# Spreading the range tests of the weights over a pair's turns on ScalarE, with a fourth raw buffer

## Chip, cores and metric

The kernel runs on one core of a Trainium2 chip. The metric is the device time of one execution in microseconds, as the median of several runs. A core has five engines that run at the same time and wait for each other by semaphores: PE (matrix multiply), VectorE (DVE in the profile), ScalarE (ACT), GpSimd (POOL) and SyncE (SP), which here only issues DMAs.

## The reference

Two blocks follow each other. The first is attention with routing: every query and every key is given to the nearest of 16 centroids of its head, and a query sees only the keys of its own cluster. The second is a feed-forward layer with a sigmoid approximation of GELU.

```python
# q, k, v: (4, 8, 768, 64); centroids: (8, 16, 64)
q_assign = argmax(einsum('bhsd,hcd->bhsc', q_n, c_n), axis=-1)
k_assign = argmax(einsum('bhsd,hcd->bhsc', k_n, c_n), axis=-1)
mask = q_assign[:, :, :, None] == k_assign[:, :, None, :]
scores = where(mask, scale * matmul(q, k.T), -1e9)
attn = softmax(scores)
x = matmul(attn, v)                     # bridged to (3072, 512)
h = x @ w_in                            # w_in: (512, 2048)
g = h * (1 / (1 + exp(-1.702 * h)))
return g @ w_out                        # w_out: (2048, 512)
```

The weights are given as 64-bit floating-point numbers; q, k, v and the centroids as 32-bit ones.

## The kernel before

The order of all work on every engine is written out by hand in program order: nothing is reordered. The tile layer adds the semaphores, and a tile's buffer is used again when all readers and writers of its former content are done.

**The attention stage** goes over 16 pairs of heads. A pair has two halves of 384 queries, and a half has six key tiles of 128 keys; a *unit* `u` is one key tile of one half, for both heads of the pair. The main loop takes two units in a *turn* `t`. So there are 96 turns, three to a half and six to a pair (`TG = 3`), and two more that finish. In the text a turn's number is `t % 6`, its place in the pair. In a turn, on each engine in this order:

- PE: `scores` of the turn's units (L467) into the PSUM tiles `s`, of which there are as many as a turn needs; `part` (L490, L481 in the first pair), which adds the cluster codes held in `rows`; then `values` (L532) of the turn before; in turns 1 and 4 the row sums (L549); in turn 1 the distances of the next pair to the centroids (`prep_near`, L343).
- ScalarE: `exps` (L498), the exponentials of `s` into `A`; then `check` (L584, L586, in turns 2 and 5), which tests the reciprocals of the row sums; then the copies of the output out of PSUM (L541, in turns 0 and 3); then, where a weight chunk was made in this turn, its test.
- VectorE: the transposes of q and k of the next pair (L322, turn 0), one addition of `A` to the row sums (L509, turn 0), the normalisation of a half (L559 to L571, turns 1 and 4), the cluster assignment of the next pair (L366 to L403), and the weight rounding (L189 to L207).
- GpSimd: the other additions of `A` to the row sums (L516), four instructions to most turns.
- SP: the loads of q and k (`in`, L134), v (L144) and the weights (`raw`, L170), the spreading of the cluster codes over rows (L412, L418), and stores of finished tiles (`kept`, L575).

The scores of the next turn overwrite `s`, so they wait for the exponentials of this turn. `A` has four buffers, each read by PE (L532) and added to the row sums.

**The weights** come in 32 chunks of 128 x 512 numbers. `rounding` turns a chunk from its raw 64-bit form into 32-bit floating point in five VectorE instructions (`steps = (0, 0, 0, 5, 0, 5)`: one whole chunk in turns 3 and 5 of a pair, besides three chunks in turns 3, 4 and 5 of the first pair). It begins with the load of the chunk two further on. It ends with `check_w`, the range test: two ScalarE instructions, a square with a sum along the row (L231) and an exponential of it with a second sum (L234). Each issues one more, short instruction that reads the accumulator. Their results go to a scratch tile `z` and are of no use; the sums go to `row_sums`. For 31 chunks `z` is the place of the last chunk in `w_out`, which is not written yet; for the last chunk it is every second word of the raw tile itself. Raw tiles have three buffers. At the end of the kernel the sums decide whether a general version must run after it; with these inputs it does not.

**The feed-forward stage** (from about 347 us) multiplies in block forms that save products. Its tiles take the memory of the attention's pools, which `att.close()` sets free; the first to be written is `G`, by a ScalarE copy (L855).

Of the kernel before, what the change touches and what calls it, by code (L numbers as in the profile page):

```python
# [8 lines left out]
FP32 = mybir.dt.float32  # L9
# [4 lines left out]
AF = mybir.ActivationFunctionType  # L14
# [24 lines left out]
def fast(  # L39
# [26 lines left out]
    nc = tc.nc  # L66
# [28 lines left out]
        name="spill", bufs=1, space=bass.MemoryType.DRAM))  # L95
# [1 line left out]
    ctx.enter_context(tc.manual_schedule())  # L97

    att = ExitStack()
    wp = att.enter_context(tc.tile_pool(name="wp", bufs=3))  # L100
    inp = att.enter_context(tc.tile_pool(name="inp", bufs=3))
    pairs = att.enter_context(tc.tile_pool(name="pairs", bufs=2))
    asg = att.enter_context(tc.tile_pool(name="asg", bufs=2))
# [5 lines left out]
        name="dram", bufs=2, space=bass.MemoryType.DRAM))  # L109
# [3 lines left out]
    def bank():  # L113
        return ps_m.tile([P, 512], FP32, name="m")
# [26 lines left out]
    def load_v(p):  # L141
# [16 lines left out]
    w_chunks = [  # L158
        (w[:, c, n:n + WN],
         src.bitcast(I32)[c * P:(c + 1) * P, 2 * n:2 * (n + WN)])  # L160
        for w, src, n_c, n_n in ((w_in, moe_w_in, NCH, DF),
                                 (w_out, moe_w_out, NF, DM))
        for n in range(0, n_n, WN) for c in range(n_c)]
    NW = len(w_chunks)
    w_raw, w_pow = {}, {}

    def load_w(i):
        if i < NW:
            t = wp.tile([P, WN, 2], I32, name="raw")
            nc.sync.dma_start(out=t.rearrange("p n t -> p (n t)"),  # L170
                              in_=w_chunks[i][1])
            w_raw[i] = t
# [7 lines left out]
    def rounding():  # L180


        i = w_done[0]
        load_w(i + 2)
        raw, w = w_raw.pop(i), w_chunks[i][0]
        e = wp.tile([P, WN], I32, name="e", bufs=2)
        a = bank()
        hi, lo, a_i = raw[:, :, 1], raw.bitcast(U32)[:, :, 0], a.bitcast(I32)
        nc.vector.tensor_scalar(out=a_i, in0=hi, scalar1=3, scalar2=0x3FFFFFF8,  # L189
                                op0=ALU.logical_shift_left,  # L190
                                op1=ALU.bitwise_and)
        yield
        nc.vector.scalar_tensor_tensor(out=a_i, in0=hi, scalar=ODD, in1=a_i,
                                       op0=ALU.bitwise_and, op1=ALU.bitwise_or)
        yield
        nc.vector.tensor_scalar(out=e, in0=a_i, scalar1=POWER, scalar2=None,
                                op0=ALU.bitwise_and)
        yield
        e = e.bitcast(FP32)
        nc.vector.scalar_tensor_tensor(out=e, in0=lo, scalar=2.0 ** -52, in1=e,  # L200
                                       op0=ALU.mult, op1=ALU.mult)
        yield
        if i >= NW // 2:
            w, a, e = (w.rearrange("p (n r t) -> p r n t", r=P // SQ, t=SQ),
                       *(x.rearrange("p (r n t) -> p r n t", r=P // SQ, t=SQ)
                         for x in (a, e)))
        nc.vector.tensor_tensor(out=w, in0=a, in1=e, op=ALU.add)  # L207

        check_w(i, raw, w_chunks[NW - 1][0] if i < NW - 1 else raw.bitcast(
            FP32)[:, :, 1])  # L210
        w_done[0] += 1
        yield

# [2 lines left out]
    def step():  # L216

        if not now and w_done[0] < NW:
            now.append(rounding())
        if now:  # L220
            n = w_done[0]
            next(now[0])
            if w_done[0] > n:
                now.clear()

    def check_w(i, raw, z):

        nc.scalar.activation(out=z, in_=raw.bitcast(FP32)[:, :, 1],  # L231
                             func=AF.Square,
                             accum_out=row_sums[:, 2, i:i + 1])
        nc.scalar.activation(out=z, in_=z, func=AF.Exp, scale=-2.0 ** 12,  # L234
                             bias=fifteen[:, 0:1],
                             accum_out=row_sums[:, 3, i:i + 1])

    load_qk(1, 0)
    load_v(0)
# [7 lines left out]
    half, fifteen, top, css, cnorm, crec = (  # L247
        consts[:, i:i + 1] for i in range(6))
# [20 lines left out]
    row_sums = const.tile([P, 4, NW], FP32, name="sums")  # L269
# [19 lines left out]
    def keep_busy(n):  # L289
        for _ in range(n):  # L290
            nc.tensor.matmul(
                out=idle[:, 0, :], lhsT=ident_h,
                rhs=ident_h[:, None, :].broadcast_to((P, 4, P)),
                start=True, stop=True)
# [5 lines left out]
    for a in range(2):  # L300
        rows = slice(a * D, (a + 1) * D)
        nc.vector.tensor_copy(
            out=cT[rows, :, a, :],
            in_=cps[rows, 0:P].rearrange("d (h a c) -> d h a c", a=2,
                                         c=NC)[:, :, a, :])
# [154 lines left out]
    def scores(u):  # L460
        g, kt = divmod(u, NJ)
        p, h = split(g)
        ps = ps_s.tile([P, 2, 512], FP32, name="s")
        for a in range(2):
            rows = slice(a * D, (a + 1) * D)
            for c in range(0, P, D):
                nc.tensor.matmul(  # L467
                    out=ps[c:c + D, a, 0:HALF],
                    lhsT=T[p, 1][rows, kt * P + c:kt * P + c + D],
                    rhs=T[p, 0][rows, h * HALF:(h + 1) * HALF],  # L470
                    start=True, stop=False)
        s_of[u] = ps[:, :, 0:HALF]

    def part(u):

        g, kt = divmod(u, NJ)
        p, h = split(g)
        if p == 0:
            for a in range(2):
                r = SQ * a  # L480
                nc.tensor.matmul(  # L481
                    out=s_of[u][:, a, :],
                    lhsT=hots[1][r:r + NC, kt * P:(kt + 1) * P],
                    rhs=hots[0][r:r + NC, h * HALF:(h + 1) * HALF],
                    start=False, stop=True)
            return
        for a in range(2):
            rows = slice(a * D, (a + 1) * D)
            for c in range(0, P, D):
                nc.tensor.matmul(  # L490
                    out=s_of[u][c:c + D, a, :],
                    lhsT=rows_of[1, p % 2][rows, kt * P + c:kt * P + c + D],
                    rhs=rows_of[0, p % 2][rows, h * HALF:(h + 1) * HALF],
                    start=False, stop=True)
# [85 lines left out]
    def check(g):  # L580


        rec = recs.pop(g)
        nc.scalar.activation(out=rec, in_=rec, func=AF.Copy,  # L584
                             accum_out=row_sums[:, 0, g:g + 1])
        nc.scalar.activation(out=rec, in_=rec, func=AF.Relu, bias=top[:, 0:1],  # L586
                             scale=-2.0 * LIMIT * LIMIT,
                             accum_out=row_sums[:, 1, g:g + 1])
# [49 lines left out]
    TG = NJ // 2  # L638

    prep_at = {}  # L640
    for p in range(1, NPAIR):
        for i in range(2 if p == 1 else 0, len(PREP)):
            t = 2 * TG * (p - 1) + (0, 0, 0, 0, 1, 2, 2)[i]
# [5 lines left out]
    def prep(p, i):  # L649
        if i == 2 and p:  # L650
            load_v(p)
        PREP[i](p)
        if i in (1, 3) and loads:
            load_qk(*loads.popleft())
# [9 lines left out]
    for t in range(NT + 2):  # L664
        us = range(2 * t, 2 * t + 2) if t < NT else ()
        for u in us:
            scores(u)
        if t == 0:
            keep_busy(6)
            prep(0, 6)  # L670
            keep_busy(4)
        for u in us:
            part(u)
        for u in us:
            exps(u)
        if recs:
            check(*recs)
        for u in us:
            add_up(u)
        if t == NT - 1:  # L680
            sums_w(0)
            sums_w(1)
        work = sorted(prep_at.get(t, ()), key=lambda w: PREP[w[1]] != prep_near)
        turns = [w for w in work if w[1] < 4]
        for p, i in turns:
            prep(p, i)
        work = [w for w in work if w[1] >= 4]
        while later:
            later.pop()()
        if 1 <= t <= NT:  # L690
            for u in range(2 * t - 2, 2 * t):
                values(u)
        if t >= 2 and (t - 2) % TG == TG - 1:
            row_sums_of((t - 2) // TG)
        while work and PREP[work[0][1]] == prep_near:
            prep(*work.pop(0))
        if t >= NT - 8 and t < NT:
            XT = list(next(made))
        for p, i in work:
            prep(p, i)  # L700
        for _ in range(0 if t in (0, 1, 2, NT - 1) else 5 if t == 4 else
                       steps[t % (2 * TG)]):
            step()
        if t >= 2 and (t - 2) % TG == TG - 1:
            normalise((t - 2) // TG)
    check(*recs)
    att.close()


# [277 lines left out]
    for b in range(B):  # L987
# [18 lines left out]
        if b < B - 1:  # L1006
            for h in range(2):
                for hp in range(HP):
                    x = xT_of[b + 1, h, hp] = xp.tile([P, HALF], FP32,
                                                      name="x")  # L1010
# [491 lines left out]
```

## Time and profile before

| | |
|---|---|
| three runs | 909.20, 909.56, 909.67 us; median 909.56 |
| the profiled execution | 909.0 us, its span 907.1 us |
| PE | 887.9 us busy, 98% of the span |
| VectorE | 728.6 us, 80% |
| GpSimd | 492.3 us, 54% |
| ScalarE | 363.4 us, 40% |
| granted clock of PE | 0.996 |
| attention stage, 58.6 to 140.8 us | of 82.2 us: PE 81.7, VectorE 75.1, GpSimd 75.6, ScalarE 58.1 |
| range tests, chunks 0 to 30 | L231: 31 of mean 688 ns; L234: 31 of mean 722 ns |
| range test, chunk 31, in place | L231: 709 ns; L234: 769 ns |

The span runs from the first to the last instruction; the execution's own time has some 1.9 us around it. Matmuls are pipelined and their ends are modelled, so a PE that is busy for 98% of the span can still be held up by others: whether it is can be read from the chain of waits, which goes back from the last instruction to what released it, step by step. A timeline lists one engine's instructions with their start, their length, and, in brackets, how long the engine was idle before and what ended the idle time.

### The profile page before, as it was taken

To read this page: it belongs to the slowest core of one execution; us is meant where nothing else is said; L and a number is where in the kernel's file an instruction comes from. 1 tells how busy PE (TensorE), PEld (TensorE's weight loads), DVE (VectorE), ACT (ScalarE), POOL (GpSimd) and SP (SyncE) were. 2 spreads that over 40 slices of the span, in tenths; PEclk is the share of its full clock that TensorE was granted. 3 is DMA by queue.
4 is the path that set the end of the run, shared out by engine and by line. 5 is a ranking of instruction groups with operands and counts; after the bars stand their busy time and mean duration, and the time that the engine had idled before them with its cause. 6 is when DMAs were issued, how large, how long until landed. Compare 5 with 4: busy or idle time off the path is not lost.

```text
span 907.1 us, 17734 instructions
## 1 busy us (share of the span) xinstructions
PE 887.9 (98%) x6712; PEld 578.1 (64%) x6712; DVE 728.6 (80%) x1170; ACT 363.4 (40%) x816; POOL 492.3 (54%) x469
## 2 busy tenths in 40 slices
PE   8999999999999999999999999999999999999995
PEld 3444444444444445557996557997557997557994
DVE  4999999998899997998898556797556797556894
ACT  3767767777676773322111232112232112232110
POOL 5899889998999998694275221143221143220120
PEclk9999999999999999999999999999999999999998
DMA  9465556666565210036213202322202322200323
GB/s 182 119 122 110 102 119 131 143 138 132 125 142 121 85 43 18 0 117 232 70 53 106 52 1 70 102 63 98 52 1 70 104 56 103 52 1 1 104 58 86
DMA packets 177565, 78.97 MB, mean 87 GB/s; under 512 B 154440, under 2 KB 160704, under 8 KB 177472
## 3 DMA queue, kind: packets, MB, share of 16 engines
q1 hardware_dynamic: 176912, 77.63, 35.0%
q8 instruction: 55, 0.90, 0.4%
q14 instruction: 38, 0.31, 0.1%
q10 hardware_dynamic: 560, 0.13, 0.1%
HBM read 61.03 MB, written 16.70 MB: 86 GB/s over the span
## 4 chain that ended last, share of the span: by engine, by line
PE 81%; DVE 9%; DMA 3%; issue 2%; SPq 2%; ACT 2%; POOL 0%; ACTq 0%; DVEq 0%
PE b L845 32%; PE b L895 23%; PE s L467 11%; PE o L532 9%; PE m L549 3%; PE s L490 2%; DVE G L593 2%; DVE E L593 1%; ACT A L498 1%; DMA raw<-in_moe_w_out_dram 1%; SPq L418 1%; DVE Tx L593 1%; PE m L343 1%; DMA raw<-in_moe_w_in_dram 1%; DMA line<-row 1%
## 5 line engine op out<-in xcount | busy, mean ns | idle before, releaser
L516 POOL TENSOR_TENSOR sum<-sum,A 128x384 f32<-128x384 f32 x252 | 264.0, 1082 | 35.4 <-ACT A L498 21.3
L836 DVE TENSOR_TENSOR G<-b,G 128x384 f32<-128x384 f32 x224 | 123.1, 556 | 99.0 <-PE b L845 89.4
L498 ACT ACTIVATE A<-s 128x768 f32<-128x768 f32 x192 | 144.7, 803 | 94.0 <-PE s L490 77.9
L593 POOL TENSOR_TENSOR Y<-y,Y 128x768 f32<-128x768 f32 x28 | 67.4, 2422 | 175.0 <-DVE y L836 151.0
L467 PE MATMUL s<-T,T 64*64 64x384 f32 x1536 | 144.6, 491 | 2.6 <-ACT A L498 0.9
L850 ACT ACTIVATE G<-G 128x384 f32<-128x384 f32 x128 | 66.3, 523 | 199.1 <-DVE G L836 197.5
L532 PE MATMUL o<-A,inv 64*64 64x384 f32 x1536 | 141.4, 483 | 0.0
L593 POOL TENSOR_TENSOR W<-w_in 128x256 f32<-128x256 f32 x32 | 23.5, 735 | 164.0 <-PE b L845 163.6
L593 DVE TENSOR_TENSOR G<-G 128x768 f32<-128x768 f32 (+1 forms) x92 | 104.1, 1155 | 0.0
L467 PEld LDWEIGHTS s<-T,T 64*64 64x64 f32 x1536 | 52.1, 132 | 78.9 <-ACT A L498 51.9
L845 PE MATMUL b<-x,W 128*128 128x384 f32 x256 | 93.0, 486 | 0.0
L845 PE MATMUL b<-Tx,w_in 128*128 128x384 f32 x256 | 93.0, 486 | 0.0
L845 PE MATMUL b<-x,w_in 128*128 128x384 f32 x256 | 88.5, 486 | 0.0
L532 PEld LDWEIGHTS o<-A,inv 64*64 64x64 f32 x1536 | 59.0, 133 | 37.9 <-issue 32.6
L845 PEld LDWEIGHTS b<-x,W 128*128 128x128 f32 x256 | 48.6, 190 | 33.9
L845 PEld LDWEIGHTS b<-Tx,w_in 128*128 128x128 f32 x256 | 48.6, 190 | 33.9
L845 PEld LDWEIGHTS b<-x,w_in 128*128 128x128 f32 x256 | 48.5, 190 | 33.5 <-issue 0.6
L895 PE MATMUL b<-G,w_out 128*128 128x192 f32 x320 | 55.9, 326 | 0.0
L895 PEld LDWEIGHTS b<-G,w_out 128*128 128x128 f32 x320 | 52.7, 190 | 1.1
L895 PE MATMUL b<-E,Wz 128*128 128x192 f32 x288 | 51.5, 328 | 1.4 <-DVE E L593 1.4
L895 PEld LDWEIGHTS b<-E,Wz 128*128 128x128 f32 x288 | 47.1, 190 | 3.4 <-POOL Wz L593 1.3
L845 PE MATMUL b<-Tx,W 128*128 128x384 f32 x128 | 46.6, 487 | 1.5 <-DVE Tx L593 1.5
(169 smaller groups left out, 1357.5 us busy)
## 6 DMA issues: line engine op xcount, KB each, us to landing
Wz<-kept_w SPq DMA_DIRECT2D x78, 256.0 KB
raw<-in_moe_w_in_dram SPq DMA_DIRECT2D x16, 512.0 KB
raw<-in_moe_w_out_dram SPq DMA_DIRECT2D x16, 512.0 KB
inv<-in_v_dram SPq DMA_DIRECT2D x16, 384.0 KB
in<-in_q_dram SPq DMA_DIRECT2D x60, 96.0 KB
in<-in_k_dram SPq DMA_DIRECT2D x60, 96.0 KB
kept<-x SPq DMA_DIRECT2D x24, 192.0 KB
x<-kept SPq DMA_DIRECT2D x24, 192.0 KB
```

What stands on the lines that cost most here:

```text
L343: nc.tensor.matmul(out=ps[r:r + SQ, w * NJ * SQ:(w + 1) * NJ * SQ] .rearrange("p (j t) -> p j t", t=SQ), lhsT=cT[:, p % HP].rearrange("p a ...
L467: nc.tensor.matmul(out=ps[c:c + D, a, 0:HALF], lhsT=T[p, 1][rows, kt * P + c:kt * P + c + D], rhs=T[p, 0][rows, h * HALF:(h + 1) * HALF], ...
L490: nc.tensor.matmul(out=s_of[u][c:c + D, a, :], lhsT=rows_of[1, p % 2][rows, kt * P + c:kt * P + c + D], rhs=rows_of[0, p % 2][rows, h * HA ...
L498: nc.scalar.activation(out=A_of[u], in_=s_of.pop(u), func=AF.Exp, scale=SCALE)
L516: nc.gpsimd.tensor_tensor(out=sum_of[g][:, a], in0=(A_of[u - 1] if kt == 1 else sum_of[g])[:, a], in1=A_of[u][:, a], op=ALU.add)
L532: nc.tensor.matmul(out=o_of[g][a * D:(a + 1) * D, r, 0:HALF], lhsT=v_in[p][rows, a, kt, :], rhs=A[rows, a, :], start=(kt == 0), stop=(kt = ...
L549: nc.tensor.matmul(out=ps[a * D:(a + 1) * D, 0:HALF], lhsT=twos, rhs=sm[:, a, :], start=(i == 0), stop=(i == len(parts) - 1))
L593: engine.tensor_tensor(out=o, in0=a, in1=b, op=(ALU.add if op == "+" else ALU.subtract))
L836: nc.vector.tensor_tensor(out=o, in0=p, in1=a, op=ALU.add)
L845: nc.tensor.matmul(out=ps[:, 0:HALF], lhsT=a[:, c], rhs=x(c), start=(c == 0), stop=(c == 1))
L850: nc.scalar.activation(out=g, in_=g, func=AF.Gelu_apprx_sigmoid, scale=2.0)
L895: nc.tensor.matmul(out=ps, lhsT=A[n][:, f], rhs=M[n][:, f], start=start and f == 0, stop=(f == FQ - 1), skip_group_check=True)
```

## The change

The tests are no longer issued where a chunk is finished. `check_w` puts its two instructions as two entries into a queue, `tests`. After the rounding steps of a turn, one entry is taken from it and issued, in turns 1, 2, 3 and 5 of a pair. What is left at the end of the attention loop is issued after the last check. All chunks now use the raw tile's own words as scratch, and raw tiles have four buffers.

```diff
-    wp = att.enter_context(tc.tile_pool(name="wp", bufs=3))
+    wp = att.enter_context(tc.tile_pool(name="wp", bufs=4))
...
-        check_w(i, raw, w_chunks[NW - 1][0] if i < NW - 1 else raw.bitcast(
-            FP32)[:, :, 1])
+        check_w(i, raw, raw.bitcast(FP32)[:, :, 1])
...
-        nc.scalar.activation(out=z, in_=raw.bitcast(FP32)[:, :, 1],
-                             func=AF.Square,
-                             accum_out=row_sums[:, 2, i:i + 1])
-        nc.scalar.activation(out=z, in_=z, func=AF.Exp, scale=-2.0 ** 12,
-                             bias=fifteen[:, 0:1],
-                             accum_out=row_sums[:, 3, i:i + 1])
+        tests.append(lambda: nc.scalar.activation(
+            out=z, in_=raw.bitcast(FP32)[:, :, 1], func=AF.Square,
+            accum_out=row_sums[:, 2, i:i + 1]))
+        tests.append(lambda: nc.scalar.activation(
+            out=z, in_=z, func=AF.Exp, scale=-2.0 ** 12,
+            bias=fifteen[:, 0:1], accum_out=row_sums[:, 3, i:i + 1]))
+
+    tests = deque()
...
+        if tests and t % (2 * TG) in (1, 2, 3, 5):
+            tests.popleft()()
         if t >= 2 and (t - 2) % TG == TG - 1:
             normalise((t - 2) // TG)
     check(*recs)
+    while tests:
+        tests.popleft()()
     att.close()
```

By the order of the built program, from the second pair on the first entry of a chunk made in turn 3 is issued in turn 1 of the next pair and the second in turn 2; of a chunk made in turn 5, in turns 3 and 5 of the next pair. The last chunk's two entries are issued in the second of the two finishing turns and after the last check. A new raw tile waits until both tests of the tile that had its buffer are done.

## The prediction

> **What bounds the kernel now.** I read the busy table, then the stages, then the chain of waits. The busy table gives PE 98% of the span and ScalarE 40%, but a modelled PE busy time says nothing of short stalls, so the chain of waits decides. In the attention stage (0 to 346.7 us) it is PE almost throughout, repeating every 20.56 us, a pair's six turns. From 112 to 123 us:
>
> ```profile
> by line: PE s L467 39.3%; PE o L532 32.1%; PE s L490 10.5%; PE m L549 7.2%; ACT A L498 6.4%; issue 4.6%; ACT w_out L234 1.7%; ACTq L498 0.2%
> ...
> 117.21 1.29 PE s L467 x16
> 118.50 0.34 PE s L490 x8
> ...
> 118.88 0.44 issue
> 119.32 0.19 ACT w_out L234
> 119.51 0.70 ACT A L498
> 120.21 0.04 issue
> 120.26 1.58 PE s L467 x16
> ```
>
> PE turns follow one another with no gap, except here: the chain leaves PE, runs through a range test (L234) and an exponential (L498), and comes back. Without it the scores would start at 118.50 + 0.34 + 1.29 (the value matmuls, L532) = 120.13 us; they start at 120.26 and take 1.58 instead of 1.29 us, since their second half waits too. **Loss: 0.13 + 0.29 = 0.42 us**, once per pair. ScalarE's timeline over the same stretch says why:
>
> ```profile
> 108.07 0.19 ACT L586 ACTIVATION_READ_ACCUMULATOR few<-few,consts 128x1 f32 x1
> 109.09 1.51 ACT L498 ACTIVATE A<-s 128x768 f32<-128x768 f32 x2 [0.83 <-POOL sum L516]
> ...
> 112.82 1.49 ACT L498 ACTIVATE A<-s 128x768 f32<-128x768 f32 x2
> 115.86 1.51 ACT L498 ACTIVATE A<-s 128x768 f32<-128x768 f32 x2 [1.55 <-PE s L490]
> ...
> 117.90 0.67 ACT L231 ACTIVATE w_out<-raw 128x512 f32<-128x512 f32 x1
> ...
> 119.32 0.19 ACT L234 ACTIVATION_READ_ACCUMULATOR w_out<-w_out,consts 128x1 f32 x1
> 119.42 1.49 ACT L498 ACTIVATE A<-s 128x768 f32<-128x768 f32 x2
> ```
>
> The two tests of turn 5 fill 117.90 to 119.42, 1.52 us, and turn 0's exponentials queue behind them. Those could have begun once their score part was there. At 115.86 the gap is ended by PE L490, which PE's timeline starts at 115.42: 0.44 us from that start to the exponential. L490 of the stalled turn starts at 118.32 there, so the exponentials were ready at 118.76 and began at 119.42.
>
> **What the Trainium skill says.** "TensorE: Matmul & The Clock Gate", Architectural detail: ScalarE and VectorE take instructions strictly in order. The trace agrees: ready exponentials wait 0.66 us behind a test. "Perfetto Trace Analysis", Optimizing Scalar/DVE Operations: if ScalarE is not saturated but makes bubbles on other engines, breaking up instructions may help; the trace has that picture, with ScalarE busy for 58.1 of the 82.2 us from 58.6 to 140.8. "SBUF — State Buffer", The DMA port swizzle: a stride inside a 16-byte line is free, for fp32 up to 4 elements; the tests will now write every second fp32. The trace has one such pair, for the last chunk: 709 and 769 ns, against mean 688 and 722 ns of the others. Nearly free.
>
> **The change part by part.** No test is added or removed: 64 in both. The built order has the same instructions in the same order on PE, VectorE, GpSimd and SP; only ScalarE's differs.
>
> (a) Turn 5 now has one test after its check. From the end of the check at 117.90 the second kind takes 112.82 - 112.10 = 0.72 us, plus 0.05 for the strided write: done at 118.67, before 118.76. The stall of 0.42 goes; at 120.13 PE is late for nothing, since the first exponential ends 118.76 + 0.8 = 119.56.
>
> (b) The three other places. Turn 1: a square, into a ScalarE gap of 3.08 us: nothing. Turn 2: after the check ScalarE idles 0.83 us up to 109.09; the test fills 108.26 to 109.03. If that cover went, the turn's exponentials would be late, but the next scores (chain: 110.44) need the first only then: it ends at 109.9, a slack of 0.5. Turn 3: the square alone ends at about 112.1 instead of 112.82; the exponentials are ready at 111.55 + 0.44 = 111.99. They come 0.7 us sooner, and GpSimd's wait for them goes (0.85 us at 113.76 in its timeline). All nothing on PE.
>
> (c) Loads. A raw buffer is now free a turn or more later, against one more buffer. By the built order, the load of each pair's second chunk waits for turn 5's test, so SP holds it until about 118.7 in the numbers above. Queued behind it on SP are the loads of k, v and q; the first waits for the transposes that VectorE starts at 120.17 and is not delayed. The held load is read a pair later, 15 us on. Nothing.
>
> (d) How often. The stall stands in the chain at 58.59, 79.14, ... 325.90 us: 14 pairs; at 38.05 the scores take 1.56, another 0.27; at the last chunk the tests wait for VectorE and the scores at 339.67 come about 0.35 late. Sum if nothing else binds: 0.27 + 14 x 0.42 + 0.35 = 6.5 us.
>
> (e) What is late next. VectorE waits 1.19 us per pair for the row sums (L559), so a pair 0.42 shorter leaves it 0.77; GpSimd idles 0.96 + 0.18 + 0.85. In the steady pairs neither binds. At both ends GpSimd does; its timeline near the start:
>
> ```profile
> 42.72 8.04 POOL L516 TENSOR_TENSOR sum<-sum,A 128x384 f32<-128x384 f32 x8 [2.60 <-DVE sum L509]
> 50.73 2.41 POOL L516 TENSOR_TENSOR sum<-A 128x384 f32<-128x384 f32 x2
> 53.10 8.54 POOL L516 TENSOR_TENSOR sum<-sum,A 128x384 f32<-128x384 f32 x8
> ```
>
> and, in its timeline at the end of the stage,
>
> ```profile
> 329.48 9.19 POOL L516 TENSOR_TENSOR sum<-sum,A 128x384 f32<-128x384 f32 x8 [0.96 <-ACT A L498]
> 338.62 2.74 POOL L516 TENSOR_TENSOR sum<-A 128x384 f32<-128x384 f32 x2
> 341.33 4.51 POOL L516 TENSOR_TENSOR sum<-sum,A 128x384 f32<-128x384 f32 x4
> ```
>
> From 42.72, set by a VectorE that is behind since the start, GpSimd runs without a gap to 61.64, and PE's row sums start at 61.71 (PE's timeline). PE cannot arrive earlier: of 0.27 + 0.42 there, 0.1 is kept. At the end GpSimd runs from 329.48 to 345.84 without a gap; its start follows VectorE's L509 (ends 329.33), which works without waiting from 309.4. The last row sums cannot come sooner, so the last pair's 0.42 and the 0.35 are lost. **Kept: 0.1 + 12 x 0.42 = 5.1 us.** The cluster codes' rows (L418) arrived late once: PE waits at 242.01, and that pair is 20.6 us long too. A pair like that keeps its length without the tests; I take off 0.1 for the chance of one: 5.0.
>
> (f) The end of attention. The last chunk's tests go behind the last turn's copies (345.07) and the last check (ends 349.04), 0.85 and 0.8 us; the first copy of the feed-forward, queued behind them, starts at 352.00 and waits by then for a store of the attention's last tile. Hidden by 2 us; if that cover went, VectorE's first addition (352.51) would be late by up to 0.8.
>
> Unknown: the in-place write when both operands are strided and VectorE and DMA are busy. Between 0.05 us less (the odd chunk needs no other tile) and 0.1 us more per test; I take 0.05 more, which moves nothing by (a) and (b).
>
> The profiled execution took 909.0 us, span 907.1 and 1.9 around it. The sum gives 909.0 - 5.0 = 904.0; the median of the runs is 909.56, 0.56 above, so in its terms **904.5 us**.
>
> **The rivals.**
> 1. GpSimd and VectorE, 90% and more busy here, take up the gain in every pair, not just at the ends. For: VectorE is 19.37 of 20.56 us busy without a gap, and its fp32 operations take 0.53 to 0.95 us for the same line, so their overlap with GpSimd may shift against it. Against: 0.77 us of slack remain. If 0.2 of each 0.42 went: 12 x 0.22 + 0.1 = 2.7 us, 906.8. Chance 0.13.
> 2. The change doesn't do what it says: the test left in turn 5 still meets the exponentials, since 118.67 against 118.76 is only 0.09. Being late by 0.2 would still cost nothing, the second scores half having about that slack. Only a check that starts later by 0.5 brings it back: 909. Chance 0.05.
> 3. Slower: the in-place tests. In turns 2 and 5 a test stands straight after a check and before exponentials. If a test took over 1.3 us in place of 0.8, the 0.5 of slack in turn 2 would be gone, and from 1.5 on turns 2 and 5 would both stall: at 1.7 us 0.4 + 0.5 a pair, 0.9 against the 0.42 of today, 14 x 0.48 = 6.7 us, 916. For: almost all tests change their output's stride. Against: the one in-place pair in the trace. Chance 0.06.
> 4. All is kept, the ends too, because GpSimd and VectorE run faster once the two collide less: 6.5 us, 903.0. Chance 0.1.
>
> **How the numbers follow.** My forecast has 0.66; its own range, 0.35 to 0.45 per pair and 10 to 13 pairs plus 0.1, is 3.6 to 6.0 us, 903.5 to 906.0. To hold 8 in 10 it reaches to rivals 4 and 1: 902.8 to 907.0. Some 0.2%, 1.8 us, is what a measurement here tells from none. Faster: 0.66 + 0.1 + 0.12 of rival 1 = 0.88; within: 0.01 + 0.05 = 0.06; slower: 0.06.
>
> **What would show it.** Right: pairs of 20.14 us in the chain of waits, no L234 in it between scores; exponentials of turn 0 that wait for PE; GpSimd's 0.85 us gap gone; VectorE's wait for the row sums down to about 0.77; PE waiting for GpSimd near 61 us and before 346 us, by 0.6 and 1 us. Wrong: pairs still at 20.5 us, a test of over 1 us, or a wait on SP that reaches a transpose.

## The result, and the profile after

| | before | after |
|---|---|---|
| median of 6 runs each | 909.62 us (909.20 to 910.79) | 903.85 us (902.80 to 905.66) |
| ratio, 95% interval | | 0.9942 (0.9932 to 0.9951) |
| the profiled execution, its span | 909.0, 907.1 us | 905.66, 903.8 us |
| a pair in the middle of the attention stage | 20.55 to 20.57 us | 20.13 us |
| first scores (L467, after: L468) to first feed-forward matmul | 335.47 us | 331.04 us |
| feed-forward stage to the end | 560.42 us | 560.86 us |

The change saves 0.6%: some 5.3 us by the ratio, while the two medians differ by 5.8. The profiled execution of the changed kernel is the slowest of its six; a second profiled execution of the same program, shown below, took 903.05 us. In the line numbers of after, most of the attention loop stands one line further down (L467 is now L468, L498 is L499, L516 is L517), and the two tests are L230 and L233.

From the page of after, the busy table and the shares of the whole chain of waits by engine:

```profile
PE 885.9 (98%) x6712; PEld 581.7 (64%) x6712; DVE 728.1 (81%) x1170; ACT 365.0 (40%) x816; POOL 499.2 (55%) x469
...
PE 88%; DVE 6%; issue 2%; POOL 2%; DMA 1%; SPq 0%; ACT 0%; DVEq 0%; POOLq 0%
```

The busy table hardly differs from before: PE is again busy for 98%. The chain tells more. Its share of PE is 88% where it was 81%, and ScalarE, 2% before, rounds to 0%. POOL has come in at 2%, of which more below.

The same stretch as in the prediction, 112 to 123 us, in the chain of waits of after (start, length, work):

```profile
by line: PE o L533 46.7%; PE s L468 36.6%; PE s L491 10.5%; PE m L550 7.2%
...
117.33 1.29 PE s L468 x16
118.62 0.33 PE s L491 x8
118.94 1.29 PE o L533 x16
120.23 1.29 PE s L468 x16
```

The chain no longer leaves PE: the value matmuls L533 follow `part` (L491), and the scores L468 after them take 1.29 us, not 1.58. And ScalarE's timeline there:

```profile
111.38 0.70 ACT L230 ACTIVATE raw<-raw 128x512 f32<-128x512 f32 x1
...
112.12 1.51 ACT L499 ACTIVATE A<-s 128x768 f32<-128x768 f32 x2
...
117.95 0.19 ACT L587 ACTIVATION_READ_ACCUMULATOR few<-few,consts 128x1 f32 x1
118.04 0.76 ACT L233 ACTIVATE raw<-raw,consts 128x512 f32<-128x512 f32 x1
...
118.88 1.52 ACT L499 ACTIVATE A<-s 128x768 f32<-128x768 f32 x2
```

One test, not two, stands between the check (L587) and the exponentials (L499). They begin at 118.88, 0.26 us after `part` (L491) starts in the chain at 118.62; before, that distance was 0.92 us (118.50 to 119.42). By (a) of the prediction, exponentials that find ScalarE free begin 0.26 us after that start (118.76 against 118.50), so these are not held up at all.

**What it adds up to.** Eleven pairs (3 to 11, 13 and 14) last 20.13 us in place of 20.55 to 20.60, 0.43 less each: 4.7 us. Pair 1 gains 0.18 and pair 12 gains 0.08; pair 2 loses 0.48 and pair 15 loses 0.26. Sum: 4.7 + 0.18 + 0.08 - 0.48 - 0.26 = 4.2 us, against 335.47 - 331.04 = 4.4 for the stage from its first scores (pair 0 lasts 23.75 us in both; the finish, behind pair 15's last value matmuls, is 0.16 shorter).

### The profile page after: what moved, and what is told of

Read it like the earlier page. It is cut to its first block, busy times and chain, and to the rows that moved or that the text cites. A ratio compares the mean times of both kernels' runs of the same rounds, so it can differ in the third digit from the quotient of the medians.

```text
span 903.8 us, 17747 instructions
## 1 busy us (share of the span) xinstructions
PE 885.9 (98%) x6712; PEld 581.7 (64%) x6712; DVE 728.1 (81%) x1170; ACT 365.0 (40%) x816; POOL 499.2 (55%) x469
## 4 chain that ended last, share of the span: by engine, by line
PE 88%; DVE 6%; issue 2%; POOL 2%; DMA 1%; SPq 0%; ACT 0%; DVEq 0%; POOLq 0%
PE b L850 32%; PE b L900 23%; PE s L468 13%; PE o L533 12%; PE m L550 3%; PE s L491 3%; DVE G L594 2%; POOL sum L517 2%; DVE E L594 1%; PE m L344 1%; DVE Tx L594 1%; DMA in<-in_k_dram 1%; DVE y L841 0%; PE o L292 0%; DMA Wz<-kept_w 0%
## 5 line engine op out<-in xcount | busy, mean ns | idle before, releaser
L517 POOL TENSOR_TENSOR sum<-sum,A 128x384 f32<-128x384 f32 x252 | 265.9, 1091 | 26.7 <-ACT A L499 16.0
L499 ACT ACTIVATE A<-s 128x768 f32<-128x768 f32 x192 | 146.2, 808 | 91.8 <-PE s L491 73.0
L468 PE MATMUL s<-T,T 64*64 64x384 f32 x1536 | 143.0, 487 | 0.7 <-ACT A L499 0.7
L533 PE MATMUL o<-A,inv 64*64 64x384 f32 x1536 | 141.4, 483 | 0.0
L468 PEld LDWEIGHTS s<-T,T 64*64 64x64 f32 x1536 | 55.2, 132 | 69.9 <-ACT A L499 36.4
L533 PEld LDWEIGHTS o<-A,inv 64*64 64x64 f32 x1536 | 59.1, 133 | 37.9 <-issue 32.8
```

What stands on the lines that cost most here:

```text
L468: nc.tensor.matmul(out=ps[c:c + D, a, 0:HALF], lhsT=T[p, 1][rows, kt * P + c:kt * P + c + D], rhs=T[p, 0][rows, h * HALF:(h + 1) * HALF], ...
L499: nc.scalar.activation(out=A_of[u], in_=s_of.pop(u), func=AF.Exp, scale=SCALE)
L517: nc.gpsimd.tensor_tensor(out=sum_of[g][:, a], in0=(A_of[u - 1] if kt == 1 else sum_of[g])[:, a], in1=A_of[u][:, a], op=ALU.add)
L533: nc.tensor.matmul(out=o_of[g][a * D:(a + 1) * D, r, 0:HALF], lhsT=v_in[p][rows, a, kt, :], rhs=A[rows, a, :], start=(kt == 0), stop=(kt = ...
```

## The experiments

All are compared with the kernel before on the same chip. The pair is a middle one in the profile of the run. "Stage" is first scores to first feed-forward matmul.

| kernel | us, median | ratio to before, 95% | pair | stage |
|---|---|---|---|---|
| four buffers alone | 908.93 | 0.9992 (0.9982 to 1.0001) | 20.56 | 335.43 |
| in place, both tests at once | 921.21 | 1.0135 (1.0115 to 1.0155) | 21.13 | 347.16 |
| after, two tests in turn 5 | 909.86 | 1.0006 (0.9998 to 1.0014) | 20.63 | 336.19 |
| after without the tests | 903.63 | 0.9938 (0.9926 to 0.9950) | 20.13 | 329.53 |
| after, two in turn 1 and two in turn 4 | 903.48 | 0.9935 (0.9921 to 0.9950) | 20.13 | 329.67 |
| after, turn 4 in place of turn 5 | 903.86 | 0.9933 (0.9919 to 0.9947) | 20.13 | 331.10 |
| after, GpSimd takes one addition | 903.58 | 0.9932 (0.9917 to 0.9946) | 20.13 | 329.94 |
| after with three buffers | 1017.72 | 1.1189 (1.1168 to 1.1209) | 28 to 30 | 444.31 |
| after, once more | 904.44 | 0.9946 (0.9933 to 0.9960) | 20.13 | 330.12 |
| two in 1 and 4, and one addition | 903.53 | 0.9935 (0.9921 to 0.9948) | 20.13 | 329.51 |
| after, old scratch | 904.68 | 0.9948 (0.9935 to 0.9962) | 20.13 | 331.07 |

### One part alone: four raw buffers

```diff
-    wp = att.enter_context(tc.tile_pool(name="wp", bufs=3))
+    wp = att.enter_context(tc.tile_pool(name="wp", bufs=4))
```

> The kernel before with four raw buffers in place of three, and nothing else. Theory (two tests in turn 5 hold up the exponentials of turn 0 on ScalarE): the same as before, 909.6 us within 1 us, and pairs of 20.56 us with the range test L231/L234 still in the chain of waits. Rival (the fourth buffer brings the gain, by loads that come free of the tests): 904 to 906 us and pairs near 20.1 us.

908.93 us, a ratio whose interval holds 1, and pairs of 20.56 us. The fourth buffer gains nothing by itself.

### One part alone: in place, but both tests at once

The kernel before with only the scratch changed.

```diff
-        check_w(i, raw, w_chunks[NW - 1][0] if i < NW - 1 else raw.bitcast(
-            FP32)[:, :, 1])
+        check_w(i, raw, raw.bitcast(FP32)[:, :, 1])
```

> The kernel before with every chunk's test writing into the raw tile itself, both tests still issued at once in turns 3 and 5, three buffers. Theory: the first test in turn 5 now waits for VectorE's second rounding step (L193, which in the profile of before ends at 118.07, the check at 117.90), and each test is some 0.03 to 0.05 us longer: the exponentials come 0.2 to 0.3 us later than before, 14 times, 912 to 914 us. Rival (writing in place is what brings the gain, since the scratch in w_out is in the way): below 907 us.

921.21 us: slower, as expected, but by 12 us and not by some 2.5 to 4.5. In ScalarE's timeline of this kernel the first test of turn 5 is held up (the bracket gives the idle time and what ended it):

```profile
122.71 0.70 ACT L230 ACTIVATE raw<-raw 128x512 f32<-128x512 f32 x1 [0.40 <-DVE m L193]
```

Its chain of waits runs through that place:

```profile
121.98 0.71 DVE m L193
...
122.71 0.79 ACT raw L230 x2
...
124.39 0.70 ACT A L497
...
125.14 1.58 PE s L466 x16
```

A test that overwrites the words which VectorE's rounding still reads (L193) has to wait for that reader. Before, its output lay elsewhere, and it waited for nothing of the kind. The chain goes on from PE's row sums over VectorE's normalisation and rounding to the test and back to PE, and does so again in the next pair: a loop, where I had reckoned with a single delay. The stall is 21.13 - 20.13 = 1.0 us per pair, against 0.42 before. So writing in place costs nothing here only if the test comes late enough, and the queue, which puts it into the next pair, sees to that.

### Two tests together again, in turn 5

After, with one entry in turns 1 and 2 and two in turn 5.

```diff
-        if tests and t % (2 * TG) in (1, 2, 3, 5):
-            tests.popleft()()
+        for _ in range((0, 1, 1, 0, 0, 2)[t % (2 * TG)]):
+            if tests:
+                tests.popleft()()
```

> The changed kernel, but the queue gives its tests in turns 1 and 2 (one each) and 5 (two), none in turn 3. Theory: turn 5 has its 1.5 us of tests again, so the stall of 0.42 us per pair is back: 908.5 to 910.5 us, pairs of 20.5 us. Rival (the gain comes from turn 3, where the exponentials go earlier and GpSimd's wait of 0.85 us goes): 903.5 to 905.5 us.

909.86 us, no different from before (ratio 1.0006), and pairs of 20.63 us, 0.50 over those of after. The chain of waits of this kernel has the picture of before again:

```profile
119.19 0.19 ACT raw L233
119.38 0.70 ACT A L499
...
120.12 1.58 PE s L468 x16
```

One pair of tests in this place takes back all that the change brought, with queue, scratch and buffers left as they are. That is the test of the cause: in the steady pairs it is the stall behind turn 5, and nothing else.

### No tests at all

After with the two tests left out of every chunk; the sums they would fill are set to zero.

```diff
-        check_w(i, raw, raw.bitcast(FP32)[:, :, 1])
         w_done[0] += 1
...
+    nc.gpsimd.memset(row_sums, 0.0)
```

> The changed kernel without any range test of the weights; their sums are set to zero once at the start, so this leaves the tests' work out. Theory: ScalarE's load as such costs nothing once turn 5 is freed, so this gains nothing over the changed kernel: 903 to 904.5 us, pairs of 20.13 us, and PE still waits for GpSimd near 62 us. Rival (ScalarE's total work bounds the stage): 898 to 901 us.

903.63 us, pairs of 20.13 us. The changed kernel is no slower than one without tests by more than these intervals resolve: 0.9942 (0.9932 to 0.9951) against 0.9938 (0.9926 to 0.9950). In the steady pairs 64 tests cost nothing any more.

### Two at once, but in turns 1 and 4

```diff
-        if tests and t % (2 * TG) in (1, 2, 3, 5):
-            tests.popleft()()
+        for _ in range((0, 2, 0, 0, 2, 0)[t % (2 * TG)]):
+            if tests:
+                tests.popleft()()
```

> The changed kernel, but the queue gives two tests at once in turn 1 and two at once in turn 4, none elsewhere. Theory (it matters only whether a test stands between exponentials that are ready and the scores that wait for them): turn 1 has a ScalarE gap of some 2.4 to 3.1 us and turn 4 one of about 2.3 us, so two tests (1.5 us) fit into each and nothing is lost: 903 to 905 us, pairs of 20.13 us. Rival (one test at a time is what counts): the pairs of 20.5 us are back, 908 to 910 us.

903.48 us and pairs of 20.13 us, although both tests run in one go as in the kernel before. In ScalarE's timeline of this kernel the exponentials after a double test (which ends at 112.5 us) wait for PE:

```profile
113.31 1.51 ACT L499 ACTIVATE A<-s 128x768 f32<-128x768 f32 x2 [0.79 <-PE s L491]
```

So that two tests run together is no harm in itself. What hurt was two tests in turn 5, where the check stands ahead of them.

### Turn 4 in place of turn 5

```diff
-        if tests and t % (2 * TG) in (1, 2, 3, 5):
+        if tests and t % (2 * TG) in (1, 2, 3, 4):
```

> The changed kernel, but with one test in each of turns 1, 2, 3 and 4 in place of 1, 2, 3 and 5. Theory: turn 5 had 0.09 us of room left at most, turn 4 has over 1 us; since the room left does not show on PE, the same as the changed kernel, 903 to 905 us and pairs of 20.13 us, with turn 0's exponentials waiting for PE's score part and not for a test. Rival (turn 5 still costs something in the changed kernel): 0.1 us a pair less, 901.5 to 902.5 us.

903.86 us, pairs of 20.13 us. The exponentials of turn 0, without any test ahead of them, now wait 0.77 us for PE, and nothing is gained by it. The single test that the change leaves in turn 5 is free.

### GpSimd takes one of VectorE's additions

This is on the early loss. In the third half of the stage (`g == 2`) all additions to the row sums go to GpSimd, so that it doesn't wait there for a VectorE that is behind.

```diff
-        if kt == 1 and g % 2 == 0:
+        if kt == 1 and g % 2 == 0 and g != 2:
```

> The changed kernel with one edit: the first addition of row sums of the second pair (L510 for g = 2, one VectorE instruction of 0.92 us) goes to GpSimd (two of 1.0 us), which waits 4.04 us for it in the profile of the changed kernel. Theory of the lost part (GpSimd, held back by a VectorE that is behind since the start, delays the row sums near 62 us by 0.9 us): GpSimd is some 2 us earlier there, the wait goes, the second pair takes 20.13 to 20.25 instead of 21.03 us: 902.8 to 903.4 us. Rival (the loss there has another cause, such as the early loads): 903.9 us as before and a second pair of 21 us.

Pair 2 lasts 20.13 us in place of 21.03, and pair 1 stays at 20.23. In GpSimd's timeline the sums of that half begin without a wait:

```profile
38.78 2.46 POOL L517 TENSOR_TENSOR sum<-A 128x384 f32<-128x384 f32 x2
```

In after they begin at 43.70 us, after 4.04 us of waiting for VectorE's L510 (shown below). The early loss is thus GpSimd's wait for VectorE. The time of the whole kernel, 903.58 us, is a little above what was expected and does not part from that of after (ratio 0.9932 against 0.9942, the intervals overlap): the gain of 0.9 us in that profile is at the edge of what the runs resolve.

### Three buffers with the queue

```diff
-    wp = att.enter_context(tc.tile_pool(name="wp", bufs=4))
+    wp = att.enter_context(tc.tile_pool(name="wp", bufs=3))
```

> The changed kernel with three raw buffers in place of four. Theory: by the built order the load of a pair's second chunk then waits for a test that is issued in turn 2 of the next pair; SP is held until then, the loads of k, v and q behind it go out some 9 us later, and then the spreading of the cluster codes behind those, some 2 us late against a room of about 1 us: PE waits for the rows, 1 to 3 us in most pairs, 918 to 945 us. Rival (the fourth buffer is not needed, the loads have a pair's time to spare): 903 to 905 us.

1017.72 us: 12% slower, far beyond the 918 to 945 us that I had expected. SP's timeline of this kernel shows the loads that it issues (start, time at the head of the queue):

```profile
117.87 15.20 SPq L170 DMA_DIRECT2D raw<-in_moe_w_in_dram  x2
133.16 3.65 SPq L134 DMA_DIRECT2D in<-in_k_dram  x4
...
137.57 4.76 SPq L134 DMA_DIRECT2D in<-in_q_dram  x4
142.43 1.90 SPq L413 DMA_DIRECT2D line<-row  x4
```

The load of a raw tile stands at the head of SP's queue for 15.2 us (two issues), until the tests of the tile that had its buffer are done. Then k, v and q follow, 9.2 us of issuing, and only then the cluster codes (L413), on which PE's `part` waits. Among the waits between 100 and 300 us PE's own entry is

```profile
PE s L491 <- DMA rows<-line: 43.8, 14, 6.5
```

that is 43.8 us in 14 waits, some 6.3 us for each of about 7 pairs (one wait of 4.7 to 6.5 us and a shorter one after it); I had reckoned with 1 to 3. Then comes a second loss, in the chain of waits after such a stall:

```profile
119.73 2.56 PE o L533 x16
122.29 2.56 PE s L468 x16
...
125.27 1.29 PE o L533 x16
```

The two groups after the stall take 2.56 us each in place of 1.29, another 2.5 us. 6.3 + 2.5 = 8.8 us per pair agrees with pairs of 28 to 30 us against 20.13. The mean granted clock of this run is 0.952 (after: 0.995). "TensorE: Matmul & The Clock Gate", HAM oscillation, of the Trainium skill describes just this: a wait for DMA of more than about 3.4 us lowers the clock to half, and the next matmuls start slow. The trace agrees: after the waits of 4.7 to 6.5 us comes a factor of 2.56 / 1.29 = 2.0, and in the stretch shown the granted clock is 0.50 from 118.9 to 124.3 us. At which length of wait the drop begins was not tried here.

So the fourth buffer, worth nothing alone, is what the queue needs.

### The changed kernel once more

This kernel has no edit: it is the changed kernel in a second set of runs.

> The changed kernel once more, unaltered, for a second profile and to stand on the same chip as the next two. Both theories: about 903.9 us. If the 0.9 us that PE loses in the second pair and the 0.9 us in the last one belong to the order of work (a test in turn 3 shifts GpSimd against VectorE), they show again, and first scores to feed-forward take 331 us; if they were chance of one execution (as the late first load was, 0.66 us), they do not.

904.44 us. In its profiled execution pair 2 lasts 20.28 us, not 21.03, and the stage 330.12 us, not 331.04. The loss at the end is smaller too: from pair 15's first scores to the feed-forward it takes 23.83 us, against 24.12 in after and 24.02 before. So part of what both ends lost belonged to that one execution. The program is the same; the difference in pair 2 goes back to one VectorE instruction. VectorE's timeline in after:

```profile
32.11 1.54 DVE L200 SCALAR_TENSOR_TENSOR e<-raw,e 128x512 f32<-128x512 uint32 x1
```

and the same instruction in the second execution:

```profile
30.32 0.69 DVE L200 SCALAR_TENSOR_TENSOR e<-raw,e 128x512 f32<-128x512 uint32 x1
```

VectorE works without a gap there, so the 0.85 us carry over to L510, for which GpSimd waits: it resumes 31.82 us after the first scores in after (at 43.70) and 30.95 us after them in the second execution. Other profiles agree: where L200 takes 1.52 to 1.55 us (after, turn 4 in place of turn 5, old scratch), pair 2 lasts 20.91 to 21.06 us; where it takes 0.69 (this execution, no tests, two in turns 1 and 4), 20.22 to 20.28. And where GpSimd takes the addition, L200 takes 1.54 us as well, but pair 2 only 20.13: the slow instruction costs time only through the addition that follows it on VectorE. What makes L200 slow is in the last section.

### Two in turns 1 and 4 together with the addition

The edits of those two experiments in one kernel.

```diff
-        if kt == 1 and g % 2 == 0:
+        if kt == 1 and g % 2 == 0 and g != 2:
...
-        if tests and t % (2 * TG) in (1, 2, 3, 5):
-            tests.popleft()()
+        for _ in range((0, 2, 0, 0, 2, 0)[t % (2 * TG)]):
+            if tests:
+                tests.popleft()()
```

> Two tests at once in turns 1 and 4, and GpSimd takes the first sum of the second pair. Theory: the two remedies for the lost part meet at the same place near 62 us, and only the one without a test in turn 3 also helps the last pair: from the first scores to the feed-forward 329.4 to 329.8 us, against 331.0 of the changed kernel and 329.7 and 329.9 of each alone; 902.4 to 903.2 us. Rival (they add up, as if at different places): 328.3 us between these points, 901.5 to 902 us.

Pairs of 20.13 us from the second on, but for the last one at 21.48, and a stage of 329.51 us, inside the 329.4 to 329.8 expected and as short as without any test (329.53). The time is 903.53 us, above the 902.4 to 903.2 expected; it is lower than both kernels in the median and clearly below the kernel before (0.9935); from the changed kernel (904.44 on the same chip) the intervals don't part it. The two gains don't add up in the measured time.

### The old scratch with the queue

```diff
-        check_w(i, raw, raw.bitcast(FP32)[:, :, 1])
+        check_w(i, raw, w_chunks[NW - 1][0] if i < NW - 3 else raw.bitcast(
+            FP32)[:, :, 1])
```

> The changed kernel with the scratch of chunks 0 to 28 back in the last chunk's place in w_out, contiguous, and only the last three chunks in place. Theory: writing in place is no part of the gain, it only makes the later issue possible for the last chunks; tests are 0.03 to 0.05 us shorter and nothing waits for that: 903.3 to 904.3 us, pairs of 20.13 us. Rival (in-place writing saves a wait or a conflict): 905 us or more.

904.68 us (0.9948), pairs of 20.13 us and a stage of 331.07, as in after. The time is 0.4 us above what was expected, but the changed kernel on the same chip took 904.44. Where the tests write makes no difference once they are spread.

## Why the prediction was right, point by point

Forecast 904.5 us (902.8 to 907.0) with 0.88 for faster; measured 903.85 us.

**(a) The stall of turn 5, right.** Predicted 0.42 us per pair and pairs of 20.14 us; measured 0.43 and 20.13. Two tests there bring the stall back, none there gains nothing more.

**(b) The other places, right.** The exponentials of turn 3 follow the single square at 112.12 us; GpSimd's gap of 0.85 us is gone. The in-place tests take 695 and 764 ns in the median, against 682 and 722 of before: 13 and 42 ns more, where I took 50. Rival 3 needed 1.3 us.

**(c) The loads, right, but not explored far enough.** With four buffers SP's wait for a test reaches 3.0 us at most, and no transpose is late. I named k, v and q as what is queued behind; the run with three buffers shows that the cluster codes behind those are what PE would miss first.

**(d) How often, nearly right.** Twelve steady pairs at 0.42 were predicted; eleven show 0.43. The twelfth is pair 12: its codes came late, its `part` waited, and it lasted 20.48 us. For the chance of such a pair I had taken off 0.1 us; it cost 0.35. It is hardly chance: the same pair lasts 20.70 us in the second execution, 20.66 with the old scratch and 20.52 with turn 4 in place of turn 5, but 20.23 without the tests. Why the codes are late just there stays open.

**(e) The ends, right in place, off in size.** Early: I expected PE to wait for GpSimd near 61 us by about 0.6. GpSimd's timeline in after:

```profile
43.70 8.07 POOL L517 TENSOR_TENSOR sum<-sum,A 128x384 f32<-128x384 f32 x8 [4.04 <-DVE sum L510]
51.72 2.42 POOL L517 TENSOR_TENSOR sum<-A 128x384 f32<-128x384 f32 x2
54.10 8.53 POOL L517 TENSOR_TENSOR sum<-sum,A 128x384 f32<-128x384 f32 x8
```

It runs without a gap from 43.70 to 62.6, and PE's row sums (L550), begun at 61.85, end at 63.54. Pair 2 is 0.90 us over 20.13 in this execution and 0.15 in the second; the mis-sized term took the start of GpSimd from the one execution of before, while it hangs on a VectorE instruction that can be 0.69 or 1.5 us. At the end of the stage, GpSimd again:

```profile
305.35 8.06 POOL L517 TENSOR_TENSOR sum<-sum,A 128x384 f32<-128x384 f32 x8 [1.62 <-DVE sum L510]
...
315.76 19.14 POOL L517 TENSOR_TENSOR sum<-sum,A 128x384 f32<-128x384 f32 x16
```

From 305.35 it runs without a gap to the end of the stage at about 342 us. I had put its first effect on PE at the last row sums; it comes one half sooner: PE's row sums at 324.72 us take 1.79 us, waiting for GpSimd, so pair 15 (up to the end of its last value matmuls) lasts 21.67 us, not 21.41, and loses 0.26 beyond the predicted loss of its gain. In the second execution these row sums take 1.50 us and the pair lasts 21.38. This is the POOL share in the chain.

In the steady pairs the balance held: VectorE waits for the row sums 10.5 us from 62 to 325 us, some 13 pairs, 0.8 each; predicted 0.77. That leaves rival 1 out, and the run without tests says the same: pairs don't get shorter than 20.13 us.

**(f) The end of attention, right.** ScalarE's timeline of after there:

```profile
348.23 0.48 ACT L860 COPY G<-b 128x384 f32<-128x384 f32 x1 [2.20 <-POOL W L594]
```

The last test ends at 346.0 us and the first copy of the feed-forward waits another 2.2 us for GpSimd. Hidden, as predicted, though by other work than I named.

**The sum.** Predicted 5.0 us; the profiled execution of after shows 4.4 for the stage, the second one 335.47 - 330.12 = 5.3, and the medians 5.3 by the ratio. The profiled executions themselves, with spans of 907.1 and 903.8 us, lie only 3.3 apart: the first scores of after start 0.66 us later than before, and its feed-forward stage, which the change does not touch, takes 0.44 longer. That stage varies from 560.29 to 560.94 us over the profiles of the kernels with four buffers. The start of the first scores varies on its own, 10.1 to 11.9 us over the profiles of these kernels; it is as large as the terms that were off, so the 0.7 us between forecast and result is not put down to one of them. The mechanism was right; that the total came so close is in part luck, since the early end, pair 12, the last pair and the feed-forward were each off by some 0.3 to 0.4 us in one profile. Rival 4 (all is kept) did not happen: from pair 15's first scores to the feed-forward it took 24.02 us before, 24.12 and 23.83 in the two executions of after, and 23.76 without the tests.

## What to carry to other kernels

Before spreading work on an engine that isn't full, look for the one turn in which it stands ahead of something that the bounding engine needs; two tests cost nothing in turns 1 and 4 and 0.43 us per pair behind the check in turn 5. Work that is put off keeps its inputs alive: count the buffers, and read what stands behind the waiting load in its queue, because the price of one buffer too few was 114 us here (1017.72 against 903.85) and not a few. A gain that repeats is kept where the next engine has slack and lost at the ends of the loop, where that engine runs without a gap.

## What was unexpected of the hardware

The same VectorE instruction on the same tile (L200) took 0.69 us in one execution and 1.54 in another, while GpSimd was adding in SBUF. GpSimd's timeline at that moment, in after:

```profile
32.11 0.99 POOL L517 TENSOR_TENSOR sum<-sum,A 128x384 f32<-128x384 f32 x1
```

and in the second execution:

```profile
30.33 1.54 POOL L517 TENSOR_TENSOR sum<-sum,A 128x384 f32<-128x384 f32 x1
```

"SBUF — State Buffer", Who interferes with whom, of the Trainium skill says that a VectorE instruction with two SBUF inputs contends with a GpSimd instruction that reads SBUF, and that the loser waits until the other is done. The trace agrees. L200 reads `raw` and `e`, both in SBUF. In after it loses: GpSimd's addition, of normal length, ends at 33.1 us, and L200 ends 0.55 us later, at 33.65. In the second execution it wins: it takes 0.69 us, and the addition that started with it takes 1.54 in place of some 1.0. In the profiles of all the kernels above, every L200 over 0.8 us ends 0.55 us after an addition of GpSimd. L207, straight after it, doesn't wait (0.69 us each time, before and in both executions of after): it has only one SBUF input, `e`, since its other one, `m`, is a PSUM bank. L200 and the addition start within 0.02 us of each other in both executions; what decides between them there is not shown.

The change moves this meeting as well: from 112 us on, L200 of turn 3 took 0.92 to 0.99 us before and takes some 0.7 us after.

And a stall of PE costs more than its length: after waits of 4.7 to 6.5 us in the kernel with three buffers, the next two groups of matmuls took 2.56 us in place of 1.29.
